# Sliding-window attention and token MLP in one program: all score masks on GpSimd, key and query buffers per head group, and small matmuls between the first transposes

## The chip, the core and the metric

The kernel runs on one core of one Trainium2 chip. The metric is device time in microseconds for one execution. Three runs of the kernel before took 444.39 (the median), 444.18 and 446.07 us.

## The reference

The input is x, one sequence of 2048 tokens of 512 features, in bf16. Two layers follow, with the same weights, and each has two parts:

```
x = x + A(layernorm(x), wqkv, wo)          # sliding-window attention
x = x + B(layernorm(x), w1, b1, w2, b2)    # MLP over the tokens
```

A has 32 heads of 16 features. Query i sees key j if 0 <= i - j < 256; scores are scaled by 1/4, masked, put through a softmax and multiplied with v, and the heads go through wo. B normalises x again and mixes over the tokens: `u = gelu(einsum("bsd,sf->bdf", h, w1) + b1)` with 1792 hidden units, `y = einsum("bdf,fs->bds", u, w2) + b2`, and y is transposed back and added to x.

## The kernel before

x stays in SBUF as 16 token tiles of 128 rows. Four such tiles make a block m of 512 tokens, and 64 tokens make a "64-block"; keys and queries are counted in 64-blocks.

**Recording and order.** The kernel is recorded as a graph of operations (`Graph.op`), each with an engine, a function, what it reads and writes, and in some cases other engines that could do it (`alts`). `ORDER` is a packed list, found ahead of time by a planner, that gives for every operation its place in the program's order and which of its engines does it. `replay` goes through the list and hands out buffers from pools; `emit` works out the semaphore waits. So each engine's queue holds its operations in the order of that list, and an engine that waits holds up all that stands behind on it.

**Attention.** `qkv(m, ...)` transposes the normalised tiles of a block (on TensorE with `ident` for the first blocks, line 570, copied out by ACT or DVE at 577/579; by DMA for the others), projects keys, queries and values (line 534, a helper of all large matmuls), and copies them out. Keys go into `kbd`, which has zeros wherever a row belongs to the other head of a pair (its slots 1 and 2 are zeroed by the two memsets of line 482, on GpSimd); for m > 0 this takes a copy to `stg` (614) and a multiplication by `par`, on GpSimd or DVE, or DMAs (629). The buffers `qT` (2 slots) and `kbd` with `vb` (3 slots) are held by block: one slot has all four head groups o.

`attention(qs, nq, ...)` handles a chunk of nq 64-blocks of queries, head group by head group (eight heads each). A chunk's scores are packed into score tiles after `attention_plan`. For each score tile TensorE writes four row-tiled sets of scores (710) into four PSUM banks, ACT makes two exponentials of 128x1024 from them into `pt` (736; seven `pt` buffers), and the product with v follows on TensorE (774). Its result is transposed on DVE (794), divided (798 and 800, the latter on GpSimd or DVE), transposed again (805), and goes through wo (534) into x (816). Layer 0 has the chunks (0,4), (4,4), (8,8), (16,8), (24,8), layer 1 the chunks (0,8), (8,8), (16,8), (24,8).

**Masks.** The edges of the window are masked in one of two ways:

- on GpSimd (757): after the exponential, `pt` is multiplied in place by `ldm`, an int32 matrix of zeros and ones;
- on TensorE (721), for the score tiles that `BIASED` names: a large negative number is added to the scores in PSUM by 8 or 16 more matmuls of `sel` and `bb`, ahead of the exponential. `sel` and `bb` are made at the start by one memset (457) and twelve short DVE instructions (465 and 472).

```
BIASED = [{1: (0, 1), 2: (2, 4), 3: (2, 4)}, {}]
```

That is: in layer 0, chunk 1 has tiles 0 and 1 of each head group biased, chunks 2 and 3 have tiles 2 and 4; in layer 1 no tile is.

**Around the attention.** Layer norms take their statistics on DVE (492, 494), the power -1/2 on GpSimd (505, `rstd`) and the scaling on DVE (512, `xh_sb`). While the attention of a chunk runs, TensorE also has the projections of later blocks, wo, and the first part of the token MLP, u = xh^T w1 (`u_part`, 534, with its evictions 880 to 884); in layer 1 also y = u^T w2 of layer 0 (`y_block`, 534 and 936). What is left of u is done after the last chunk (`u_last`, 895, 906 and 910), and layer 1 ends with its own y.

**Start.** `f_warm` issues 42 matmuls of 128x128 on ones while x is loaded (395). x tiles 0 and 1 are then normalised one at a time, transposed, and projected by halves of a block.

Of the kernel before, what the change touches and what calls it, by code (L numbers as in the profile page):

```python
# [11 lines left out]
P = 128  # L12
# [3 lines left out]
    'c-p;HKZx_l6(4zLzti5$7bY-;K9~!0puiNmpaTUI(18Lf6i^|84jgdd!Urx~xX^(L6)IG?Foy~k3aD_QfD02`nBc;N3kO`daIuApEnIA|#THv^v4x9_*WO+4'  # L16
    '?zeYelH;ELNSb*wn)iFZ_j?rAF$R-hFaQl1MD2Rqc6z-ObQ9Q0I+5N0tsfxQJZ;LS!FS>l^i3OrI;cSnFmiiGyf&@5jmh6O=dO2NTm8i)OK$V|W~Nxg7^#NJ'
    'jjxzWMnhGW85~ZB!%dnDi#TCwz^U3X`=CE6K9r;3hd+J&A?k2$x9mn-Z`d_2@O-X0ys9W)ZDu~_p3arkO4F#KBpQtoqCinF!l<RHmyDTgyH(T%p_c@!H#fEo'
    'NVc*z7gx)rZQEqE`f@g-o6U?;v>FcifYR~k?(U8nMQON*e0lM;b<<dPEWE%=X9dwLoN9=Vo17!WSnl--R;v{`8+g1d*>cJ3@O|9YvQTV@`f(kFjD=AUgsre$'
    'mjA9V@Th3F+et!`s7Pp0q!H~kBfshgxY=lUp55>Wvn;<FRI61LU0q#Y-QCqLYZ$k#WABm}OV6p{>GYd_jSO=bcu3bBr;09vC~|ja!lu#fqK=_h3gbLjuXRIT'  # L20
    'a!#pfo0flZVL8syS+3A~GSdksh!<QHCs)g&$TCEfZLfz>#~TpkdUG||B%9m2+h+6bE_+|=tk>7K7_G*e%|()&uk6*#j?BWIPUot6bv2)_*K2Q>=l1z>B&XKg'
    'DyRL~yx;HJqp?r^Zjx_F+3)wVtoP?$-ox0o`(-~>Rof^i<(RQv7KT|Cwma9?##N_f7`!dZ?W!Eqo6V-Gaxd@!cT|~DS=Togx=zl|?Un7?OUKb<O`D9@OKwg$'
    '?qil?Sx)`T_iKsZPm=VbJa==KQf6B`HlsMHitSt~JG!h9g`8o_rj#1mnrfOxu!7Gf>dus*pyxPd;&??bw|cg!&;-S?5ow{JzsFe9G4C}pzhS5}U?O*xYML_R'
    '8dE5vf`XLl(`koLQ*e|6?M|uHY8uyded}y3Sw7SC1u$>c*Yh==&mq(h!o$<S_U>*7Zjp>Jl7)3rC=5s-ALRKKH=ENe&+`%3&7?8_zQ3WWtI8m5M2;{Bk^ngl'
    'u$o#GL7@4_b2+yR1^@)8FvHAj119Rkvcv#&b;cFWn8J346i_Hu$1|92=?jbMq~kh{m{1W|VJu$GCON?XqtwsUIE&-Bu4z#fQ4JHMAm5K7U*KTbwp9fHdjbMV'
    'm&;26=ks%@Y4&(V`NSIIdn>*ITkt_fc^F1#XR_REbUFyir@DR`*6Xz(2&&)LzpmFcSckGqF?3zzpPtDO%!F+@EEl#lzj2)5(CO6DG_BRTjYit&h(c>Sx^8M7'
    'htT&_)3FTz08v#!bO0e&i6l#g$OIN%rb*E4?d>%}NM9@#=bMcHSJj7;;dwe9t0PSt2wV$I^RnFc7(36h)k-OUTmGZk{ZU~GpbE0JQ?=wWjO%rs>)%n4GNv*Y'
    'Lc6t+<;M3LzFfBX`U0>1fEJ6AfmuFSET@ZtF)%La7=UrJ2}bqls8$1kBfBekI9yD1IoC9)>}SFOj}XB)>-O&;>=#KQb)_uIFt)O!i_H<nol=i1p%7CTg;_Q0'
    'R<c$%%i19boodag1MYfGvs(2;O5JL;&W8hs*K0x|8jS5K%drEYKECS%lQ^cR_49K_t6C6ZHqrg*G`PGBdIcD(*Ur_|KQ->yg7K=U8pdW5U)WKkYjLcGmTQS3'
    'Y1ok+;?~ubt{M98&jG)^k^R43se(cm4O(9<mkUbgA|q{8`Jnu6P>x0;H*hDO=eW~yOrW#SEK!i<e7-39L=mLw!SPO_I-R2YvUibQ;=EVIdEmO^F&=l_K~|=e'  # L30
    'h6%<7fr!}k_%@Dx&#hkgLCaq{#72&72SH5;RW)l?P1p5=*t%{IP=D)r)Kgs7kY)Ws5RZrsQC(8gFm6Xw9y_)xi(Uu?J2g!)Wzb@A+<>9RDO6~k)l{|sz?*Kj'
    'TQr#f{n{ZIsVtYNyqGT~!Twn~o6g`VoQy@F(QpU`Vdy2jZjx2{{Z<jhu4Q$_TV$gnhwUKsyk@<oyKW^-JvWKH7)Hp}bwg+m)OEpco3_~*L`|+jRfdoPfe^%w'
    'wS{mxxfBm~7Tv5j&AhAteYMi<RVrGaZjHw0<Kb#)>3Ugy^G%)`gP~}g3P_5qAU}XMwBN^;l{gDG-^oeXj^fDr_FLcgEVOZb&oSjc8W2DNA)>SZLZ?PIK;j7l'
    'Qr1ghFHL|@tDV{aAbYckswh+eghG(brY&u}U5oM(!bJiy8YAH(8b#T!*TsLm=vxM8Hd{?SYBZV+N-zYnnYeM1c1$OAfnkV3HUiVqEV+PyF;T;YX%Wj7osI~x'
    'u||Zr!or0s8lTYN8=WwPh{O=l-U(4|ZZH=n<VSd8;UHvwm<T-yhf_9TO!Qbfh@uFtI-M}g$E;H(JPgyc*G(tA-e?rxcGEN|Hk(l1xe3_;j?;7+;sM$1&=!f1'
    '<)9SSGVF%vL%<G9A<eqsIEI0c2*I!o3ur3P02T3LfOata684$+Jlearyrld5>~D|m-*!K&d2&8nPL78p>Evlc@pSJXZ1;co?$^9N*ZmYcsZ`!oo{jH4Pag&='
    'A3tBE@;E8pdV0U)*)gAjl>{r{{(RyG@2?O@$A0jz&(Q{llZ(;Mjy+F~A$ljBoV*C?4JeOMl)xU=hZjl@FRq*(N4$%$a)|R)^al^=kfz72KAObm=Xgc|Ns>N+'
    'VL#(@Qh95pa#E>$5{IS7xSp6LNtMIRBO9e-8t;7`;@?9Gq{r~2iX<JURC=D@r<#yHHChS$s`i^tb9?`jvz2=q9jax|s7I*3c=C9>JS}@8bEo&PL-55Hp9Ao@'
    'bfD5bxCdgtqSS$<(lL^vBq4lMf)nuKcBdR?JN?*~)QMQU7n*xzd8uE*Pd))}7s|6Lsys)ca#U=)%kF!xr=L}h)>Xg(5a}&q+)q5kBos$H?67(Fv}!-Q`;*?i'
    '+YRmp#1DcOT67PCw8u#Vzencu<mBxV1g|EghtpR+0?6y9O64)ehj1$|rMB|AmmHKtdaH`0=jsOzJbAGkNXJ?wN&i#HNv}mvdXQO3l3o&VuO5;FB<WZM_JdD)'  # L40
    '@^Ie6*zxGW@v-~8Ao)*pub+?PztWmVG5>#5{FgB4r{5%j2gDxiS@nEeiho_z{SPfNNM8'
# [52 lines left out]
class Graph:  # L94
# [4 lines left out]
    def __init__(self, nc, es):  # L99
        self.nc = nc  # L100
        self.sem = {e: es.enter_context(nc.semaphore(f"s_{e}")) for e in self.ENGS}
        self.dsem = [es.enter_context(nc.semaphore(f"s_dma{i}")) for i in range(self.NDMA)]
        self.ops = []
        self.last_w = {}
        self.readers = {}

    def op(self, eng, fn, reads=(), writes=(), cost=200.0, prio=None, dma=False, after=(), holds=(), cfg=None, cls=None,
# [197 lines left out]
def bass_interleave_layers__sliding_block__mixer_token_mlp__prompt_kernel(  # L305
# [19 lines left out]
    MASKED = 4e9  # L325
# [5 lines left out]
    BIASED = [{1: (0, 1), 2: (2, 4), 3: (2, 4)}, {}]  # L331
# [4 lines left out]
    with es:  # L336
# [22 lines left out]
        sel = sb("sel", [P, 2, P])  # L359
        bb = sb("bb", [P, 2, 4, 64])  # L360
# [17 lines left out]
        p_xhT, p_qT, p_stg = Pool("xhT", 2), Pool("qT", 2), Pool("stg", 5)  # L378
        p_kv, p_pt, p_rl, p_oT = Pool("kv", 3), Pool("pt", NPT), Pool("rl", NRL, True), Pool("oT", 2)
# [76 lines left out]

        op("gpsimd:zero", lambda e: e.memset(sel[:].rearrange("p a b -> p (a b)").bitcast(dt.float32), 0.0), writes=["sel"], cost=200)
        BIAS_KEYS = []
        for r in range(4):
            g0, g1 = 32 * r, 32 * r + 32  # L460

            def f_sel(e, g0=g0, g1=g1):
                d, v = sel[g0:g1, 0, 0:32], ident[g0:g1, g0:g1]
                (p, c), (q, _) = [[list(a) for a in x.ap] for x in (d, v)]
                return e.tensor_copy(bass.AP(d.tensor, d.offset, [p, [160, 2], [64, 2], c]),
                                     bass.AP(v.tensor, v.offset, [q, [0, 2], [0, 2], c]))
            op("vector:sel", f_sel, reads=["ident", "sel"], writes=[("sel", r)], cost=150)
            for i, (add, mul) in enumerate(((-1.0, MASKED), (0.0, -MASKED))):
                def f_bb(e, g0=g0, g1=g1, i=i, add=add, mul=mul):
                    v = tri[g0:g1, g0:g0 + 64]  # L470
                    p, c = [list(a) for a in v.ap]
                    return e.tensor_scalar(bb[g0:g1, :, 2 * i:2 * i + 2, :], bass.AP(v.tensor, v.offset, [p, [32, 2], [0, 2], c]), add, mul,  # L472
                                           op0=ALU.add, op1=ALU.mult)
# [542 lines left out]
```

## Time and profile before

| | |
|---|---|
| median of three runs | 444.39 us |
| the profiled execution: own time, span | 445.56 us, 443.6 us |
| time outside the span | 1.96 us |
| TensorE / VectorE / ScalarE / GpSimd busy | 418.5 / 307.4 / 322.7 / 201.1 us |
| mean granted TensorE clock | 0.996 |
| exponentials (736) | 304, spaced 0.93 us where they run back to back |
| layer 0's exponentials | from 11.1 to 158.5 us |
| layer 1's exponentials | from 207.0 us on; the last masks begin at 361.9 us |
| masks on GpSimd (757) | 226 instructions, 149.9 us by the groups of their shapes |
| mask matmuls on TensorE (721) | 352, from 21.7 to 117 us |

PE is TensorE, PEld its weight loads, DVE VectorE, ACT ScalarE, POOL GpSimd, SP the queue that issues DMAs. L736 is line 736 of the kernel. Matmuls overlap and their ends are modelled, so PE's busy share says less than the moment at which the next instruction starts.

### The profile page before, as it was taken

To read this page: it belongs to the slowest core of one execution; us is meant where nothing else is said; L and a number is where in the kernel's file an instruction comes from. 1 tells how busy PE (TensorE), PEld (TensorE's weight loads), DVE (VectorE), ACT (ScalarE), POOL (GpSimd) and SP (SyncE) were. 2 spreads that over 40 slices of the span, in tenths; PEclk is the share of its full clock that TensorE was granted. 3 is DMA by queue.
4 is the path that set the end of the run, shared out by engine and by line. 5 is a ranking of instruction groups with operands and counts; after the bars stand their busy time and mean duration, and the time that the engine had idled before them with its cause. 6 is when DMAs were issued, how large, how long until landed. Compare 5 with 4: busy or idle time off the path is not lost.

```text
span 443.6 us, 14491 instructions
## 1 busy us (share of the span) xinstructions
PE 418.5 (94%) x6270; PEld 193.5 (44%) x6344; DVE 307.4 (69%) x582; ACT 322.7 (73%) x372; POOL 201.1 (45%) x305
## 2 busy tenths in 40 slices
PE   7888988998999999999999999999999999999997
PEld 5554443443443444444444444444334444444443
DVE  7988879777895678664468789898887457521223
ACT  3999999999999940708989999999999980430000
POOL 3567652464577641001456686677866551000000
PEclk8999999999999999999999999999999999999999
DMA  7575504410133538451434434031211347653533
GB/s 242 153 129 91 101 16 72 77 28 18 36 83 100 122 88 249 125 168 25 99 80 104 111 73 97 17 71 38 56 45 30 105 123 202 189 158 99 167 115 105
DMA packets 94127, 44.47 MB, mean 100 GB/s; under 512 B 24304, under 2 KB 94064, under 8 KB 94064
## 3 DMA queue, kind: packets, MB, share of 16 engines
q1 hardware_dynamic: 94064, 43.55, 39.1%
q8 instruction: 50, 0.82, 0.8%
q14 instruction: 13, 0.11, 0.1%
HBM read 33.56 MB, written 2.10 MB: 80 GB/s over the span
## 4 chain that ended last, share of the span: by engine, by line
PE 79%; ACT 13%; DVE 3%; issue 2%; DMA 1%; SPq 1%; POOL 1%; POOLq 0%
PE PS L534 53%; ACT pt L736 12%; PE PS L710 9%; PE PS L895 8%; PE PS L774 8%; DMA w1b<-in_B_w_dram 1%; DVE rl L794 1%; PE PS L721 1%; DVE stats L492 1%; SPq L830 1%; PE PS L570 0%; DVE vst L649 0%; DVE bb L472 0%; DVE x_sb L816 0%; POOL rstd L505 0%
## 5 line engine op out<-in xcount | busy, mean ns | idle before, releaser
L736 ACT ACTIVATE pt<-PS 128x1024 bf16<-128x1024 f32 (+1 forms) x304 | 281.9, 1034 | 12.0 <-PE PS L710 8.0
L757 POOL TENSOR_TENSOR pt<-pt,ldm 128x256 int32<-128x256 int32 (+2 forms) x226 | 146.9, 675 | 91.7 <-ACT pt L736 91.2
L534 PE MATMUL PS<-xhT,wqkv 128*128 128x512 bf16 (+1 forms) x267 | 65.3, 362 | 4.5 <-issue 1.4
L534 PE MATMUL PS<-xh_sb,w1b 128*128 128x512 bf16 x262 | 66.0, 380 | 2.9 <-issue 1.9
L534 PE MATMUL PS<-uT,w2b 128*128 128x512 bf16 (+1 forms) x285 | 66.7, 370 | 0.8 <-issue 0.5
L710 PE MATMUL PS<-qT,kbd 32*128 32x256 bf16 (+4 forms) x1488 | 60.4, 252 | 5.6 <-ACT pt L736 2.8
L936 DVE SCALAR_TENSOR_TENSOR x_sb<-PS,b2col,x_sb 128x512 bf16<-128x512 f32 x31 | 22.4, 745 | 48.4 <-PE PS L534 48.4
L505 POOL TENSOR_TENSOR rstd<-agg,mhalf 128x2 f32<-128x2 f32 (+1 forms) x33 | 23.5, 713 | 67.8 <-DVE agg L494 67.8
L794 DVE STREAM_TRANSPOSE rl<-PS 128x1024 f32<-128x1024 f32 x32 | 39.9, 1246 | 19.8 <-PE PS L774 19.3
L710 PEld LDWEIGHTS PS<-qT,kbd 32*128 32x128 bf16 x1488 | 22.0, 93 | 63.9 <-ACT pt L736 48.2
L774 PE MATMUL PS<-pt,vb 64*17 64x320 bf16 (+4 forms) x2976 | 43.6, 252 | 1.2 <-DVE vst L649 0.5
L910 ACT ACTIVATE uT<-rl,b1col 128x512 bf16<-128x512 f32 x28 | 18.5, 713 | 36.1 <-DVE rl L906 35.7
L492 DVE BATCH_NORM_STATS2 stats<-x_sb 128x6 f32<-128x512 bf16 x64 | 42.8, 678 | 0.4
L534 PEld LDWEIGHTS PS<-uT,w2b 128*128 128x128 bf16 x294 | 27.1, 98 | 30.9 <-issue 3.7
L534 PE MATMUL PS<-uT,pt 128*128 128x512 bf16 x163 | 39.5, 380 | 0.3
L774 PEld LDWEIGHTS PS<-pt,vb 64*17 64x17 bf16 x2976 | 31.0, 85 | 17.4 <-issue 7.3
L895 PE MATMUL PS<-xh_sb,w1b 128*128 128x512 bf16 x164 | 37.0, 379 | 0.7 <-DMA w1b<-in_B_w_dram 0.6
L534 PEld LDWEIGHTS PS<-xh_sb,w1b 128*128 128x128 bf16 x280 | 23.8, 98 | 31.6 <-issue 7.0
L534 PEld LDWEIGHTS PS<-xhT,wqkv 128*128 128x128 bf16 x288 | 24.5, 99 | 28.8 <-issue 5.6
L534 PE MATMUL PS<-wqkv,xhT 128*128 128x512 bf16 x115 | 32.3, 381 | 3.5 <-issue 1.3
L534 PE MATMUL PS<-wo_sb,oT 128*128 128x512 bf16 x124 | 32.6, 380 | 0.4 <-issue 0.3
L512 DVE TENSOR_SCALAR xh_sb<-x_sb,agg,rstd 128x512 bf16<-128x512 bf16 x64 | 27.2, 445 | 3.2 <-POOL rstd L505 3.1
(64 smaller groups left out, 337.0 us busy)
## 6 DMA issues: line engine op xcount, KB each, us to landing
w1b<-in_B_w_dram SPq DMA_DIRECT2D x112, 128.0 KB, 2.7
w2b<-in_B_w_dram SPq DMA_DIRECT2D x70, 128.0 KB, 2.6
pt<-in_B_w_dram SPq DMA_DIRECT2D x42, 128.0 KB, 3.2
vb<-vst SPq DMA_DIRECT2D x64, 68.0 KB, 2.1
out_dram<-x_sb SPq DMA_DIRECT2D x15, 128.0 KB, 1.8
x_sb<-in_A_x_dram SPq DMA_DIRECT2D x3, 512.0 KB, 7.3
wqkv<-in_A_wqkv_dram SPq DMA_DIRECT2D x4, 256.0 KB, 4.5
wqkv<-in_A_wqkv_dram SPq DMA_DIRECT2D x1, 512.0 KB, 6.6
```

Of the source, the lines that this page charges most:

```text
L492: op("vector:stat", lambda e: e.bn_stats(st[:, 0:6], x_sb[:, t, :]), reads=[f"x{t}"], writes=[("st", i)], cost=dve_cost(512))
L505: op("gpsimd:rstd", lambda e: e.tensor_tensor(rstd[:, t0:t1, 0], agg[:, t0:t1, 1], mhalf[:, 0:1].to_broadcast([P, t1 - t0]), op=ALU.pow), ...
L512: op("vector:xh", lambda e: e.tensor_scalar(xh_sb[:, t, :], x_sb[:, t, :], agg[:, t, 0:1], rstd[:, t, :], op0=ALU.subtract, op1=ALU.mult), ...
L534: return e.matmul(o, lhsT=w, rhs=x, start=start, stop=stop, skip_group_check=True)
L710: last = e.matmul(bank(tt[r // 2], r % 2)[:, base + c0 * 64:base + (c0 + n) * 64], lhsT=kbd[32 * r:32 * r + 32, tk.slot, o, jj].rearrange( ...
L736: op("scalar:exp", lambda e, ts=ts, tp=tp, i=i, cols=cols: e.activation(probs(tp)[:, i, 0:cols, :], pair(ts)[:, :, 0:cols].rearrange("p r ...
L757: return e.tensor_tensor(v, v, m, op=ALU.mult)
L774: last = e.matmul(bank(t, h)[32 * r:32 * r + 17, i + q0 * 64:i + (q0 + n) * 64], lhsT=vb[64 * h:64 * h + 64, tk.slot, jj, 4 * o + r, :], r ...
L794: op("vector:od", lambda e, t=tod, tr=tr: e.transpose(rl[:, tr.slot:tr.slot + 2].rearrange("p a b -> p (a b)"), pair(t)), reads=[(tod, i) ...
L895: last = e.matmul(bank(tu, tt), lhsT=v()[:, sc - b0, k0 + tt * P:k0 + (tt + 1) * P], rhs=xh_sb[:, sc, :], start=(sc == b0), stop=(sc == NT ...
L910: op("scalar:gelu", lambda e, ft=ft, tt=tt: e.activation(uT[:, ft, :], rl[:, tmps[tt].slot], ACTF.Gelu_apprx_tanh, bias=b1col[:, ft:ft + 1 ...
L936: op("vector:resy", lambda e: e.scalar_tensor_tensor(x_sb[:, t, :], bank(ft), b2col[:, t:t + 1], x_sb[:, t, :], op0=ALU.add, op1=ALU.add), ...
```

## The change

- **Masks.** `BIASED`, `sel`, `bb`, the biased matmuls, and the memset and twelve DVE instructions that make `sel` and `bb` are gone. All score tiles are masked on GpSimd.
- **Buffers.** `qT` becomes a pool of 8 slots of one head group each, `kbd` one of 12; `vb` keeps 3 slots by block in a pool of its own. The memory is the same; a slot is free again once its own head group has been used.
- **Warm-up.** `f_warm` issues 40 matmuls instead of 42. After the transposes of x tile 0 come 2 more matmuls of the same kind, after those of tile 1 come 8 (`keep_warm`); the TensorE operation that is recorded next has to follow them.
- **Zeroing.** The two memsets of `kbd` are recorded after the first layer norms and read `xh1`, so they can't run ahead of tile 1's scaling.
- **Order.** `ORDER` is another list, for the new graph.
- In `u_part` and `u_last` two expressions are written more generally; with the splits in use they give what they gave before.

```
...
-    'c-p;HKZx_l6(4zLzti5$7bY-;K9~!0puiNmpaTUI(18Lf6i^|84jgdd!Urx~xX^(L6)IG?Foy~k3aD_QfD02`nBc;N3kO`daIuApEnIA|#THv^v4x9_*WO+4'
+    'c-qBPKZxtd86Vl>yLp`6p@Vs#g9+$h4wNtfB`84w6$%VN50s$7g$`Ue;D8DhE?l@!zyTF598lrHg$oxhT&PgtfCw%&u*DWGT)1$+g^Mj5aIuApEw;$m>s@>I'
...
+        if eng == "tensor":
+            after, self.next_pe = list(after) + self.next_pe, []
         for a in after:
             deps[a.idx] = a
...
-    BIASED = [{1: (0, 1), 2: (2, 4), 3: (2, 4)}, {}]
...
-        qT = sb("qT", [P, 2, 4, 512])
+        qT = sb("qT", [P, 8, 512])
         stg = sb("stg", [P, 5, 512])
-        kbd = sb("kbd", [P, 3, 4, 8, 2, 64])
+        kbd = sb("kbd", [P, 12, 8, 2, 64])
...
-        p_xhT, p_qT, p_stg = Pool("xhT", 2), Pool("qT", 2), Pool("stg", 5)
-        p_kv, p_pt, p_rl, p_oT = Pool("kv", 3), Pool("pt", NPT), Pool("rl", NRL, True), Pool("oT", 2)
+        p_xhT, p_qT, p_stg = Pool("xhT", 2), Pool("qT", 8), Pool("stg", 5)
+        p_k, p_v, p_pt, p_rl, p_oT = Pool("k", 12), Pool("v", 3), Pool("pt", NPT), Pool("rl", NRL, True), Pool("oT", 2)
...
-            for _ in range(42):
+            for _ in range(40):
                 last = e.matmul(PS[:, warm.slot, 0:P], lhsT=uT[:, 0, 0:P], rhs=uT[:, 0, 0:P], start=True, stop=True)
             return last
+        def keep_warm(n, after):
+            spare = Tile(banks)
+
+            def f(e):
+                for _ in range(n):
+                    last = e.matmul(PS[:, spare.slot, 0:P], lhsT=uT[:, 0, 0:P], rhs=uT[:, 0, 0:P], start=True, stop=True)
+                return last
+            g.next_pe = [op("tensor:fw", f, reads=["uT0"], writes=[spare], cost=60 * n, cfg="f", cls="f", after=after)]
...
-        op("gpsimd:zero", lambda e: e.memset(sel[:].rearrange("p a b -> p (a b)").bitcast(dt.float32), 0.0), writes=["sel"], cost=200)
...
-            op("vector:sel", f_sel, reads=["ident", "sel"], writes=[("sel", r)], cost=150)
...
-                op("vector:sel", f_bb, reads=["tri"], writes=[("bb", r, i)], cost=150)
...
-        for k in (1, 2):
-            op("gpsimd:zero", lambda e, k=k: e.memset(kbd[:, k].rearrange("p a b c d -> p (a b c d)").bitcast(dt.float32), 0.0),
-               writes=["kz0"], cost=1900)
...
+        def zero_keys():
+            for k in (1, 2):
+                op("gpsimd:zero", lambda e, k=k: e.memset(kbd[:, 4 * k:4 * k + 4].rearrange("p a b c d -> p (a b c d)").bitcast(dt.float32), 0.0),
+                   reads=["xh1"], writes=["kz0"], cost=1900)
...
-            tx, tq, tk = Tile(p_xhT), Tile(p_qT), Tile(p_kv)
+            tx, tq, tk, tv = Tile(p_xhT), [Tile(p_qT) for _ in range(4)], [Tile(p_k) for _ in range(4)], Tile(p_v)
...
+                if wide and not layer and m == 0:
+                    keep_warm((2, 8)[i], [g.ops[-1]])
...
+                if first and not layer:
+                    zero_keys()
...
-                    on_pe = su[0][0] in biased and len(su) == 1
-
-                    def f_sc(e, su=su, tt=(tA, tB), on_pe=on_pe):
-                        last, fresh = None, True
+                    def f_sc(e, su=su, tt=(tA, tB)):
...
-                        for c0, nc_, w0 in plan[su[0][0]][1] if on_pe else ():
-                            for a in range(2):
-                                lo = 32 if w0 < 2 and a else 0
-                                hi = nc_ * 64 - (32 if w0 + nc_ > 2 and not a else 0)
-                                for r in range(4):
-                                    last = e.matmul(
-                                        bank(tt[r // 2], r % 2)[:, c0 * 64 + lo:c0 * 64 + hi],
-                                        lhsT=sel[32 * r:32 * r + 32, a, :],
-                                        rhs=bb[32 * r:32 * r + 32, 1 - a].rearrange("p i n -> p (i n)")[:, w0 * 64 + lo:w0 * 64 + hi],
-                                        start=False, stop=True, tile_position=(32 * r, 0), skip_group_check=True)
...
-                    masks, mk = [] if on_pe else list(plan[su[0][0]][1]), []
+                    masks, mk = list(plan[su[0][0]][1]), []
...
```

More of the change, by code (lines that the diff above doesn't have):

```diff
@@ L609, in proj @@
                     op(two[0][0] + ":evka", two[0][1], reads=[key] + [("par", h) for h in range(2)],
-                       writes=[(tk, "k", o, h, k) for h in range(2) for k in KEYS(a, b)], cost=two[0][2], prio=-3e5, alts=two[1:])
+                       writes=[(tk[o], h, k) for h in range(2) for k in KEYS(a, b)], cost=two[0][2], prio=-3e5, alts=two[1:])
                     if wide:
@@ L619, in f_kz @@
                     got = []
-                    assert layer or m > 2 or tk.slot
+                    assert layer or m > 2 or tk[o].slot > 3
                     for h in range(2):
@@ L955, in bass_interleave_layers__sliding_block__mixer_token_mlp__prompt_kernel @@
                 phase[0] = 8 * layer + c
-                tos[c] = attention(qs, nq, tqs, tks, BIASED[layer].get(c, ()))
+                tos[c] = attention(qs, nq, tqs, tks)
                 gate.append([prev_sc[0]])
```

115 lines of the change are left out of this document (48 added, 67 removed).

## The prediction

> **What bounds the kernel now.** I read the page first, then the busy time by stages, the groups of line 721 and 757, the list of waits, and the start in order of time.
>
> ```profile
> span 443.6 us, 14491 instructions
> PE 418.5 (94%) x6270; PEld 193.5 (44%) x6344; DVE 307.4 (69%) x582; ACT 322.7 (73%) x372; POOL 201.1 (45%) x305
> ...
> ACT  3999999999999940708989999999999980430000
> POOL 3567652464577641001456686677866551000000
> ```
>
> ACT is at 9 through both attention stages and nearly empty elsewhere; POOL's 45% is an average over stages of 70% and stages of nothing. So the stages are read apart (columns: window, its length, then busy us of each engine):
>
> ```profile
> 16.00:66.00 50.00, 43.67 (x1147) 23.32 (x1157) 42.49 (x88) 47.77 (x55) 34.68 (x47) 1.00 0.46 81
> 66.00:133.00 67.00, 62.40 (x1338) 27.82 (x1350) 56.31 (x106) 65.48 (x71) 33.17 (x51) 1.00 0.25 52
> 260.00:310.00 50.00, 48.73 (x859) 21.00 (x868) 44.38 (x81) 47.26 (x52) 36.83 (x56) 1.00 0.25 53
> 286.00:297.00 11.00, 10.63 (x195) 4.74 (x190) 10.53 (x19) 9.83 (x11) 10.01 (x14) 1.00 0.36 78
> ```
>
> Layer 0's attention (16 to 133) is set by ACT: 96 to 98% busy, PE 87 to 93%. In layer 1 (260 to 310) PE is at 97% and ACT at 95%. The last row is a stretch of layer 1 in which four engines all run at 89 to 97%.
>
> ```profile
> L757 POOL TENSOR_TENSOR pt<-pt,ldm 128x256 int32<-128x256 int32 x162 | 117.8, 743 | 57.4 <-ACT pt L736 56.8
> L757 POOL TENSOR_TENSOR pt<-pt,ldm 128x128 int32<-128x128 int32 x60 | 28.2, 472 | 30.7 <-ACT pt L736 30.7
> L721 PE MATMUL PS<-bb,sel 32*128 32x96 bf16 x256 | 7.8, 201 | 0.0
> ```
>
> These groups give the prices of masks (mean ns after the comma). Of the waits, the first line is from 11 to 160 us, the second from 310 to 365, where every mask is on POOL:
>
> ```profile
> ACT pt L736 <- PE PS L721: 2.7, 9, 0.6
> ...
> PEld PS L774 <- POOL pt L757: 2.0, 5, 0.5
> ```
>
> The start: projections at 7.60 and, for comparison, twelve equal ones at 18.85; and the clock by half microseconds (PE busy, then PEclk).
>
> ```profile
> 7.60 2.74 PE L534 MATMUL PS<-xhT,wqkv 128*128 128x256 bf16 x12 [0.68 <-ACT xhT L579]
> ...
> 18.85 1.49 PE L534 MATMUL PS<-xhT,wqkv 128*128 128x256 bf16 x12
> ...
> 7.00:7.50 0.50, 0.00 (x0) 1.00 1.05 313
> 7.50:8.00 0.50, 0.40 (x3) 0.59 1.05 301
> ...
> 10.50:11.00 0.50, 0.50 (x13) 0.50 1.16 352
> 11.00:11.50 0.50, 0.50 (x6) 1.00 1.01 356
> ```
>
> The granted clock is halved from 7.59 to 11.0 us, and the first projections take 2.74 us instead of 1.49. In the chain that ended last, they stand between the copy of the transposes and ACT's first keys and exponentials, after which ACT hardly stops: its delay at the start goes to the end of layer 0's attention.
>
> **The change part by part**, against the profiled execution (span 443.6, own time 445.56, so 1.96 outside; 1.17 above the median of 444.39).
>
> (a) Small matmuls. If the clock holds, 2.74 - 1.49 = 1.25 us leave the chain. In the 3.41 us before the drop (4.18 to 7.59) PE was busy for 1.68, with no gap over 0.68. The windows row 56.2 to 59.6, 2.19 busy of 3.40, kept the full clock. The last of the 42 matmuls ran 10 in half a microsecond, so ten more make some 0.5 and two fewer in front take 0.1: about 2.1 busy, close to the row that held. Against: eight at 0.05 to 0.1 us need 0.4 to 0.8 in a gap of 0.67, so up to 0.2 late. From -1.25 to +0.2; I take -0.8. The Trainium skill, "TensorE: Matmul & The Clock Gate", Part 1, says that the clock falls after an idle window of about 3.4 us; read literally, nothing fell here for idleness and the ten matmuls are worth nothing (the sum would be 0.8 higher). The row speaks against that reading: it halved at half-busy.
>
> (b) Mask matmuls gone. 352 of them, 8 or 16 behind the scores of 24 tiles: chunk 1 has 4 x 8 + 4 x 16, chunks 2 and 3 have 8 x 16 each. From the first of 16 to the next instruction is 0.29 us (69.00 to 69.29), of 8 it is 0.19 (27.97 to 28.16): 20 x 0.29 + 4 x 0.19 = 6.6 us of PE. ACT waited 2.7 us for them in nine places; some of these waits go over to the scores themselves (line 710), so ACT gets 2.0 (from 0 to 2.7), and layer 0's attention ends that much earlier.
>
> (c) The other 4.6 of the 6.6 us count only where TensorE's later work (u, projections) is pulled into the gaps, shortening the PE-bound stretch after ACT's last exponential. PE already has 6.3 + 4.6 us of gaps from 16 to 133 that the present order leaves open. Between 0 and -4.6; half, -2.3.
>
> (d) Masks added to POOL. Chunk 1, for each of four head groups: two of 256 columns and one of 128, so 4 x (2 x 0.743 + 0.472) = 7.8 us; chunks 2 and 3: 8 tiles each with two of 256, 2 x 8 x 1.486 = 23.8. Together 44 instructions and 31.6 us. They hide beside ACT, but POOL is a strict queue: behind each mask stand `rstd`, the products (800), the key copies (629), and for them DVE's scaling and the next block's projections; PE's products with v wait for the mask itself. Price from below: in layer 1, 138 masks from 209 to 362 us cost PE's weight loads 2.4 us (the 2.0 shown, and 0.4 from 260 to 310), so 44 cost 0.8; below zero is excluded, since a mask can't come before its exponential. From above: from 16 to 66 us POOL has 34.7, and gets chunk 1's 7.8 and five tiles of chunk 2, 7.4: 49.9 of 50. It has to give its eight key copies and four products to DVE, which is at 42.5. The two together: 92.4 of 100. Layer 1 held 20.5 of 22 (93%) for 11 us, but 81.2 of 100 over 260 to 310. At the latter rate, 92.4 take 56.9 us instead of 50: +6.9. I take +1.2, near the low end, for work there isn't tied to that stretch: from 66 to 133 POOL would have 33.2 + 16.3 of 67, and key copies and statistics of blocks 2 and 3 can go there.
>
> (e) The twelve DVE instructions for `sel` and `bb` take 2.7 us, most beside the loading of x; four lie in the crowded stretch from 9.9 to 15.3. From -0.8 to 0; I take -0.3. Without that cover nothing is lost.
>
> (f) Buffers by head group, and the two memsets (1.80 us each): in the list of waits nobody waits for a slot of `qT` or `kbd`, and the memsets already start at 16.72 and 29.73, long after tile 1's scaling (6.06). Zero; if a memset is put ahead of an `rstd` or a mask, 1.8 is late once.
>
> (g) The new order reaches everywhere. In layer 1, 209 to 362, PE is idle 4.7 of 153 us: gaining more isn't in the rows, losing as much is easy. 0, with 4.7 to both sides.
>
> Sum: -0.8 - 2.0 - 2.3 + 1.2 - 0.3 = -4.2. Span 439.4, own time 441.4, median 440.2.
>
> **The rivals.**
>
> *POOL and DVE full from 16 to 66 us (slower).* Then (d) costs 6.9; of (b) and (c) only what lies outside that stretch stays, about 1.3; the start keeps 0.8. 444.4 + 6.9 - 2.1 = 449.2. It decides as soon as the two engines together can't hold 93% for 50 us. For it: DVE's own instructions get longer beside masks: `xh_sb` took 384 ns from 66 to 133 us and 509 from 260 to 310, the DVE key copy 345 and 531. The Trainium skill, "SBUF — State Buffer", "Who interferes with whom", gives such a lock between the two engines; it speaks against this change, and the rows agree. Against: the 11 us row, with PE at 97% beside it.
>
> *ACT alone sets the end (no change).* ACT's 2.7 us of waits turn into others, PE's freed time stays idle: 444.4 - 0.8 - 0.3 + 0.8 = 444.1. For it: the gaps that PE has today in a stage where ACT is at 96%. Against: the 9.6 us of u that is still done after 156 us (44 matmuls at 0.22), and could move up.
>
> *All of it is used (faster still).* -1.25 - 2.7 - 4.6 + 0.8 - 0.3 = -8.05: 436.3. It needs a filler for every gap.
>
> If the change doesn't do what it says, it is in (a): the clock falls all the same, and the forecast ends at 441.0.
>
> **How the numbers follow.** Forecast 0.49 (its own range 437.5 to 442.1), all of it used 0.13, no change 0.14, POOL and DVE full 0.24. A measurement of this kernel tells about 0.5% (2.2 us). Faster 0.62, same 0.14, slower 0.24. The range goes from 435, below the best case by a little of (g), to 449.5, just over the slow one; some 0.06 lies below and 0.12 above.
>
> **What would show it.** Right: clock 1.00 from 7.5 to 11 us, ACT's first exponential before 10.3; no L721; 270 masks and some 233 us on POOL; products and key copies of 16 to 66 us mostly on DVE; ACT's last exponential of layer 0 near 155 us; PEld waiting under 5 us for masks. Wrong: PEld or ACT waiting for masks or `rstd` by more than that before 133 us, layer 0's attention as long as before (147.4 us), or a longer layer 1, where nothing was changed but the order.

## The result, and the profile after

The changed kernel takes 445.71 us (median of 20 executions; 444.43 to 448.72), the kernel before 444.33 (443.78 to 446.07). The ratio is 1.0034, with a 95% interval from 1.0019 to 1.0048: slower by about a third of a per cent. The forecast was 440.2. The profiled execution after has an own time of 445.6 and a span of 443.8.

The page of the changed kernel, with ACT and POOL in forty slices:

```profile
span 443.8 us, 13856 instructions
PE 415.2 (94%) x5930; PEld 188.7 (43%) x6000; DVE 301.8 (68%) x557; ACT 323.3 (73%) x374; POOL 234.7 (53%) x351
...
ACT  3888999999999931637999999999999970530000
POOL 5577887677996731010665758976896651000000
```

POOL has its 33.6 us more (the forecast said 31.6), PE lost 3.3 busy us. By stages, in the windows of before (length, then busy us of PE, PEld, DVE, ACT, POOL, then the granted clock, the DMA share and GB/s):

```profile
16.00:66.00 50.00, 41.89 (x927) 19.68 (x936) 43.64 (x92) 45.73 (x54) 38.42 (x57) 1.00 0.44 94
66.00:133.00 67.00, 59.56 (x1209) 25.14 (x1211) 57.27 (x101) 66.42 (x73) 53.63 (x79) 1.00 0.33 70
260.00:310.00 50.00, 48.42 (x857) 20.68 (x865) 39.71 (x73) 48.12 (x54) 40.00 (x61) 1.00 0.23 51
286.00:297.00 11.00, 10.47 (x177) 4.43 (x176) 10.45 (x18) 10.00 (x12) 9.18 (x14) 1.00 0.40 88
```

The new order put 26 of the 44 added masks between 66 and 133 us (POOL 53.63, before 33.17) and 17 between 16 and 66. From 66 to 133 ACT is busier than before, 66.42 against 65.48. From 16 to 66 it is less busy, 45.73 against 47.77: there lies what layer 0 loses. The masks' groups, and the waits from 11 to 160 us for a mask and of ACT:

```profile
L733 POOL TENSOR_TENSOR pt<-pt,ldm 128x256 int32<-128x256 int32 x202 | 146.5, 745 | 38.9 <-ACT pt L712 38.6
...
L733 POOL TENSOR_TENSOR pt<-pt,ldm 128x128 int32<-128x128 int32 x64 | 30.1, 472 | 15.7 <-ACT pt L712 13.0 <-DVE ldm L459 2.6
```

```profile
PEld PS L750 <- POOL pt L733: 3.3, 8, 0.5
...
ACT pt L712 <- PE PS L697: 4.0, 7, 1.3
ACT qT L582 <- PE PS L520: 1.4, 1, 1.4
```

A mask costs what it did (745 and 472 ns), and TensorE waits for masks for only 3.3 us. But ACT waits 5.4 us where it waited 4.4: the 2.7 us for line 721 are gone, and waits for scores (L697) and projections (L520) of up to 1.4 us have come. At the start the clock holds:

```profile
7.06 0.60 PE L520 MATMUL PS<-xhT,wqkv 128*128 128x256 bf16 x4
8.14 1.05 PE L520 MATMUL PS<-xhT,wqkv 128*128 128x256 bf16 x8 [0.49 <-DMA wqkv<-in_A_wqkv_dram]
```

```profile
7.50:8.00 0.50, 0.15 (x2) 0.00 (x0) 0.41 (x3) 0.31 (x1) 0.24 (x1) 1.00 0.95 298
10.50:11.00 0.50, 0.50 (x6) 0.29 (x3) 0.49 (x2) 0.50 (x2) 0.19 (x1) 1.00 1.27 207
```

Twelve projections take 0.60 and 1.05 us, and the first exponential starts at 9.73 instead of 11.11. So 1.38 us are won at the start and lost again by 20 us. All engines in order of time (start, duration), shortly after:

```profile
13.54 2.12 DVE L493 TENSOR_SCALAR xh_sb<-x_sb,agg,rstd 128x512 bf16<-128x512 bf16 x1
13.70 1.80 POOL L499 MEMSET kbd<- 128x2048 f32 x1
...
15.71 0.40 PE L556 MATMUL PS<-ident,xh_sb 128*128 128x128 bf16 x4 [0.16 <-DVE xh_sb L493]
...
17.36 0.73 DVE L565 COPY xhT<-PS 128x512 bf16<-128x512 bf16 x2
...
18.15 1.05 PE L520 MATMUL PS<-xhT,wqkv 128*128 128x256 bf16 x8 [1.46 <-DVE xhT L565]
18.80 0.37 ACT L582 CAST qT<-PS 128x256 bf16<-128x256 f32 x1 [1.38 <-PE PS L520]
```

The scaling of x tile 3 takes 2.12 us; the same instruction takes 0.40 for the tile before it. It ends 0.16 us after the memset of `kbd` that started beside it. The view of busy time counts these 1.7 us as DVE's work, so no wait of DVE shows them. Transposes, their copies, the projections and ACT (idle 1.38) follow late. Later ACT waits another 1.34 us, at 32.80, for scores that stand on TensorE behind projections of block 1, whose transposes come by DMA.

The spans of the profiled executions, cut at the exponentials, put the rest in place (us, differences of rows of the timelines; "to layer 1" runs from layer 0's last exponential to layer 1's first):

| kernel | first exp. | layer 0 exp. | to layer 1 | layer 1 exp. | to the end | span |
|---|---|---|---|---|---|---|
| before | 11.11 | 147.39 | 48.54 | 154.11 | 82.45 | 443.6 |
| old order, small matmuls | 9.87 | 147.35 | 48.05 | 154.06 | 82.47 | 441.8 |
| old order, 24 tiles unmasked | 9.61 | 144.94 | 48.38 | 154.25 | 82.52 | 439.7 |
| old order, masks on POOL | 9.78 | 155.90 | 48.51 | 154.09 | 82.42 | 450.7 |
| after | 9.73 | 148.26 | 47.86 | 154.37 | 83.58 | 443.8 |
| after, memset moved | 8.97 | 146.30 | 47.86 | 154.36 | 84.11 | 441.6 |
| after, three moves (below) | 9.06 | 146.00 | 47.86 | 154.43 | 83.35 | 440.7 |

### The profile page after: what moved, and what is told of

Same layout as the page of the kernel before. It is cut to its first block, busy times and chain, and to the rows that moved or that the text cites. A ratio compares the mean times of both kernels' runs of the same rounds, so it can differ in the third digit from the quotient of the medians.

```text
span 443.8 us, 13856 instructions
## 1 busy us (share of the span) xinstructions
PE 415.2 (94%) x5930; PEld 188.7 (43%) x6000; DVE 301.8 (68%) x557; ACT 323.3 (73%) x374; POOL 234.7 (53%) x351
## 4 chain that ended last, share of the span: by engine, by line
PE 65%; ACT 21%; DVE 5%; DMA 2%; issue 2%; SPq 2%; POOL 1%; DVEq 0%
PE PS L520 46%; ACT pt L712 21%; PE PS L697 7%; PE PS L871 6%; PE PS L750 6%; DMA wqkv<-in_A_wqkv_dram 1%; POOL pt L733 1%; DVE rl L770 1%; DVE xh_sb L493 1%; SPq L818 1%; DMA w1b<-in_B_w_dram 1%; SPq L806 1%; DMA pt<-in_B_w_dram 1%; DVE rl L882 0%; DVE qT L580 0%
## 5 line engine op out<-in xcount | busy, mean ns | idle before, releaser
L733 POOL TENSOR_TENSOR pt<-pt,ldm 128x256 int32<-128x256 int32 (+2 forms) x270 | 177.2, 684 | 57.6 <-ACT pt L712 54.6
L520 PE MATMUL PS<-xhT,wqkv 128*128 128x512 bf16 (+1 forms) x273 | 64.4, 355 | 8.0 <-ACT pt L712 4.1
L520 PE MATMUL PS<-uT,w2b 128*128 128x512 bf16 (+1 forms) x285 | 69.3, 369 | 1.1 <-issue 0.5
L520 PE MATMUL PS<-xh_sb,w1b 128*128 128x512 bf16 x262 | 65.8, 380 | 3.3 <-issue 1.7
L697 PE MATMUL PS<-qT,kbd 32*128 32x256 bf16 (+4 forms) x1488 | 60.3, 251 | 5.9 <-ACT pt L712 3.0
L697 PEld LDWEIGHTS PS<-qT,kbd 32*128 32x128 bf16 x1488 | 22.0, 92 | 64.1 <-ACT pt L712 48.4
L520 PE MATMUL PS<-uT,pt 128*128 128x512 bf16 x162 | 41.4, 379 | 0.6 <-DMA pt<-in_B_w_dram 0.3
L520 PEld LDWEIGHTS PS<-uT,w2b 128*128 128x128 bf16 x294 | 26.9, 98 | 31.7 <-issue 4.0
L520 PEld LDWEIGHTS PS<-xhT,wqkv 128*128 128x128 bf16 x288 | 24.2, 97 | 34.3 <-ACT pt L712 5.7
L520 PEld LDWEIGHTS PS<-xh_sb,w1b 128*128 128x128 bf16 x280 | 23.6, 97 | 32.6 <-issue 6.4
L493 DVE TENSOR_SCALAR xh_sb<-x_sb,agg,rstd 128x512 bf16<-128x512 bf16 x64 | 32.0, 519 | 4.4 <-POOL rstd L486 4.3
L520 PE MATMUL PS<-wqkv,xhT 128*128 128x512 bf16 x117 | 31.8, 380 | 2.3 <-ACT pt L712 1.1
L520 PE MATMUL PS<-wo_sb,oT 128*128 128x512 bf16 x120 | 30.9, 380 | 1.6 <-issue 1.0
```

The lines of the kernel that those rows point to most:

```text
L493: op("vector:xh", lambda e: e.tensor_scalar(xh_sb[:, t, :], x_sb[:, t, :], agg[:, t, 0:1], rstd[:, t, :], op0=ALU.subtract, op1=ALU.mult), ...
L520: return e.matmul(o, lhsT=w, rhs=x, start=start, stop=stop, skip_group_check=True)
L697: last = e.matmul(bank(tt[r // 2], r % 2)[:, base + c0 * 64:base + (c0 + n) * 64], lhsT=kbd[32 * r:32 * r + 32, tk[0][o].slot, jj].rearran ...
L733: return e.tensor_tensor(v, v, m, op=ALU.mult)
```

## The experiments

My theory: most of the loss is the memset beside the scaling, with what follows from it. The rivals: the masks on POOL after all, and the new order in itself. In the runs on the old order, its list is kept and only what a part adds or drops is changed in it. The buffers by head group have no run of their own; they are in the run with every part. Medians are set against the kernel before on the same chip ("+" is slower).

**The parts by themselves, in the old order.** Small matmuls alone (40 in front, then 2 and 8):

```
-            for _ in range(42):
+            for _ in range(40):
+                if wide and not layer and m == 0:
+                    keep_warm((8, 2)[i], [g.ops[-1]])     # tile 1 is transposed first here
```

> The kernel before with its own order, plus the small matmuls: 40 instead of 42 at the start, 2 after the transposes that run first, 8 after those that run second. Theory A (the start is worth its time, and the new order loses it again further on): the clock stays at 1.00 from 7.5 to 11 us, the first exponential comes 1.0 to 1.4 us earlier than 11.1, and 0.8 to 1.4 us of that reach the end: 443.0 to 443.6 against 444.3. Theory B (a later start of nothing else: the gain at the start is taken up by the next wait, the weights' DMA or DVE): first exponential earlier, end within 0.4 us of before.

Measured: 444.23, -0.4 us, ratio 0.9988 (0.9978 to 0.9999). The first exponential starts at 9.87, but two kernels without small matmuls, next, start theirs at 9.61 and 9.78: the halved clock of before's profile is not in every execution. Of 99 executions of before beside these runs, 23 had a mean granted clock of 0.996 and a median time of 445.35, the other 76 had 0.999 or 1.0 and a median of 444.20.

No masks for the 24 tiles, so that the 352 mask matmuls leave and nothing comes in their place (these scores stay unmasked):

```
-                    masks, mk = [] if on_pe else list(plan[su[0][0]][1]), []
+                    masks, mk = [] if bare else list(plan[su[0][0]][1]), []   # bare: the 24 tiles; sel, bb and on_pe are gone
```

> The kernel before with its own order, with the masks of the 24 biased tiles left out altogether: no mask matmuls, no GpSimd masks for them. This is what the freed PE time is worth without any price on GpSimd. The prediction's steps (b) and (c) together were 4.3 us (0 to 7.3). If ACT alone sets the end of layer 0's attention: 0 to 2.7 us faster (ACT's waits for line 721), the rest of the 6.6 us turning into PE idle time. If PE's time counts: 4 us or more faster.

Measured: 441.71, -2.9, ratio 0.9929 (0.9914 to 0.9944). Layer 0's exponentials take 144.94 us, 2.4 less. The next stretch is no shorter (48.38).

The 24 tiles masked on POOL, each mask in the list behind the second ACT instruction after its exponentials:

```
-                    masks, mk = [] if on_pe else list(plan[su[0][0]][1]), []
+                    masks, mk = list(plan[su[0][0]][1]), []
```

> The kernel before with its own order, but the 24 tiles' masks on GpSimd: 44 mask instructions put in behind the next tile's exponentials, 352 matmuls and the 13 instructions for sel and bb left out. Theory A (masks on GpSimd are about free, the loss of the changed kernel is in its order): 443.3 to 444.8. Rival 1 (POOL and DVE full from 16 to 66 us): slower by 3 to 7 us, with waits of PE for masks and rstd there. Rival 2 (ACT alone sets the end of layer 0): within 0.7 us of before, last exponential of layer 0 still at 158 to 159.

Measured: 451.97, +7.4, ratio 1.016 (1.014 to 1.018). All engines in order of time at one of the places:

```profile
112.50 1.37 POOL L604 TENSOR_SCALAR kbd<-stg,par 128x512 bf16<-128x512 bf16 x2
...
113.83 2.79 POOL L718 TENSOR_TENSOR pt<-pt,ldm 128x256 int32<-128x256 int32 x4
...
115.39 0.93 PE L735 MATMUL PS<-pt,vb 64*17 64x64 bf16 x56 [2.07 <-POOL pt L718]
...
118.32 1.94 ACT L697 ACTIVATE pt<-PS 128x1024 bf16<-128x1024 f32 x2 [3.30 <-PE PS L682]
```

A key copy stands ahead of four masks, the product with v waits 2.07 us for one of them, the next scores stand behind that product on TensorE, and ACT is idle for 3.30. It is a burst: from 112.50 to 116.62 POOL is full, and over the whole stage it is not (45.35 us busy from 66 to 133). Behind it the granted clock is halved from about 116 to 119.4 us, so the 3.30 hold some of that as well. Of the 12.2 us that ACT waits for scores up to 168 us, 8.4 lie between 66 and 133, not from 16 to 66 where the rival had put them.

The same with the 44 masks cut to 8 of their columns (the rest of these scores stays unmasked), and, at full width, with each mask directly behind its exponential in the list:

```
-                        def f_mask(e, tp=tp, w=nc_ * 64,
+                        def f_mask(e, tp=tp, w=8 if short else nc_ * 64,
```

> b_pool with the 44 added masks cut to 8 columns each (the rest of those tiles' masks is left out): the same instructions at the same places in GpSimd's queue and the same waits, but little GpSimd time. If b_pool's 7.4 us are GpSimd's time: most of it goes, 441.7 to 443.5. If they are the extra step between exponential and product, however short: 447 or more.

> b_pool with the 44 added masks put into GpSimd's queue directly behind their own tile's exponentials, ahead of key copies and products that stood in front of them. If b_pool's loss is the place of the masks in GpSimd's queue: at least 3 us faster than b_pool's 452.0. If GpSimd has too little time in layer 0 whatever the place: within 1.5 us of b_pool, with other work late instead.

Measured: 443.07 (-1.4; 0.9962, 0.9948 to 0.9976) and 471.55 (+27.0; 1.0602, 1.0584 to 1.062). Against the kernel without these masks, 44 nearly empty instructions cost 1.5 us, their full width 8.8 more, and an earlier place in POOL's queue another 20. There, each mask holds up whatever POOL could have done while its exponential was still running: POOL waits 49.6 us for exponentials up to 175 us, against 28.0 up to 168 with the later place. Neither expectation had that. How much of the 20 is the queue and how much the clock stays open: the clock is also halved for 27 us in all, and its mean is 0.971 to 0.974 in all four executions (0.996 to 0.999 with the later place).

Every part together (masks on POOL, buffers by head group, small matmuls) in the old order:

> Every part of the change, but in the order of before: masks on GpSimd put in as in b_pool, small matmuls as in b_warm, buffers by head group. Theory A (the new order is what loses): 442.3 to 443.8, the sum of b_warm and b_pool, so 2 to 3 us less than the changed kernel's 445.7. Rival (the parts lose in any order): 445 or more.

Measured: 452.4, +7.8, ratio 1.0174 (1.0154 to 1.0193), like the masks alone. So the new order, at +1.4, has won back 6.4 of 7.8 us; as a whole it is not what loses, and the second rival is left with single places in it.

**In the new order.** The changed kernel with `masks = []` for the 24 tiles, so without its 44 added masks:

> The changed kernel with its own order, with the 44 added masks left out of GpSimd's queue (those tiles go unmasked). If the masks still cost time in the order that was found for them: 1.5 us or more faster than the changed kernel's 445.7, down to b_nomask's 441.7. If the new order hides them and loses elsewhere: 445 to 445.7.

Measured: 446.47, +2.0, ratio 1.0031 (1.0012 to 1.0051), the same as the changed kernel's 1.0034 (and above what was expected either way). In the new order the masks cost nothing that can be measured: the first rival falls for this order. The long scaling, 2.12 us beside the memset, is in this kernel too.

The second memset placed behind the next three masks, nothing else, in two runs:

```
 [rstd 2] ... [mask 0]
-[memset kbd 2]
 [mask] [mask] [mask]
+[memset kbd 2]
 [rstd 4]
```

> The changed kernel with one instruction moved: the second memset of kbd, which starts at 13.70 us while the scaling of x tile 3 on DVE (13.54) takes 2.12 us instead of 0.4, goes behind the next three masks on GpSimd (about 17.3 us). If DVE was held by the memset and that stall is on the path: the scaling is back at 0.4 us, ACT's idle time of 1.38 at 18.80 goes, and 0.8 to 1.4 us reach the end (444.3 to 444.9). If it isn't on the path: the scaling is short, the end unchanged within 0.4.

> The changed kernel with the second memset behind the next three masks, run a second time with the other three on one chip. The memset theory: again some 2 us below the changed kernel, 443.0 to 444.2. The rival, that its first runs were lucky in the clock: 445 to 446.

Measured: 443.66 (-0.85; 0.9991, 0.9964 to 1.0017) and 444.42 (+0.35; 1.0002, 0.9981 to 1.0022); in the profiled execution of the first:

```profile
12.78 0.40 DVE L493 TENSOR_SCALAR xh_sb<-x_sb,agg,rstd 128x512 bf16<-128x512 bf16 x1
...
15.69 1.81 POOL L499 MEMSET kbd<- 128x2048 f32 x1
...
15.89 1.05 PE L520 MATMUL PS<-xhT,wqkv 128*128 128x256 bf16 x8 [0.30 <-DVE xhT L565]
```

The scaling is back at 0.40, and TensorE's wait of 1.46 is 0.30. Against the changed kernel's +1.38 the move is worth 2.2 us by the medians in the first run and 1.0 in the second, whose 444.42 lies between what was expected of the theory and of the rival, and whose interval overlaps the changed kernel's. The two differ because each median falls between two groups: in both runs six of twelve executions have a lowered clock, with medians of 445.98 and 445.77, and six have 0.999 or 1.0, with 442.13 and 442.84 (the changed kernel's four of that kind: 445.43). So at full clock the move is worth more than the medians say. In the profiled pair 0.76 of the 2.2 us of span come before the moved instruction (first exponential at 8.97 instead of 9.73, without the wait for wqkv); 1.96 come off layer 0's exponentials, and 0.5 are lost at the end.

The other way round: the old order with small matmuls, and the memset placed beside a scaling:

```
-               writes=["kz0"], cost=1900)
+               reads=[("bb", 1, 0)] if k == 1 else [], writes=["kz0"], cost=1900)
```

> The kernel before with its old order and the small matmuls, and one memset of kbd moved so that it begins together with the scaling of x tile 2 (it now reads the bb entry that DVE makes just ahead of that scaling). If a memset of 1.80 us holds DVE's scaling for its whole length, as the changed kernel's record suggests, the scaling takes 1.8 to 2.1 us instead of 0.41, that tile's transposes and ACT come 1.4 to 1.7 us later, and the time is 0.8 to 1.7 us above the kernel with the small matmuls alone (444.23): 445.0 to 445.9. Rival: the 2.12 us in the changed kernel came from something else (the exponentials' reads, the DMAs); then the scaling stays near 0.41 and the time is 444.0 to 444.6.

Measured: 445.78, +1.7, ratio 1.0039 (1.0025 to 1.0053), that is 2.1 us worse than the small matmuls alone (-0.4). First this kernel, then that one:

```profile
13.49 1.98 DVE L518 TENSOR_SCALAR xh_sb<-x_sb,agg,rstd 128x512 bf16<-128x512 bf16 x1
...
13.52 1.80 POOL L488 MEMSET kbd<- 128x2048 f32 x1 [2.77 <-DVE bb L478]
...
15.39 0.70 DVE L471 COPY sel<-ident 32x128 bf16<-32x128 bf16 x1
...
18.73 0.60 ACT L744 ACTIVATE pt<-PS 128x512 bf16<-128x512 f32 x1 [1.67 <-PE PS L718]
```

```profile
13.50 0.41 DVE L518 TENSOR_SCALAR xh_sb<-x_sb,agg,rstd 128x512 bf16<-128x512 bf16 x1
...
13.82 0.18 DVE L471 COPY sel<-ident 32x128 bf16<-32x128 bf16 x1
```

One memset of 1.80 us makes this one instruction 1.57 us longer. The next on DVE, a small copy, now falls beside a mask of 0.76 us and takes 0.52 longer. Together that is 2.1 us, and so is the difference of the medians (the profiled spans differ by 1.6). The time lies where the memset theory put it, and that settles the cause of this loss: it comes about in the old order too, with the small matmuls as the only other part of the change.

**The small matmuls, and TensorE's second wait.** The changed kernel without the ten small matmuls:

```
-            for _ in range(40):
+            for _ in range(42):
-                    keep_warm((2, 8)[i], [g.ops[-1]])
```

> The changed kernel without its ten small matmuls (42 in front again, the banks handed out as in the changed kernel). If they are worth in this order what they were in the old one, the median rises by 0.4 us, to about 446.1, and the profiled record shows either a halved clock before 11 us or none. Rival from the recorded forecast: they are worth 0.8 to 1.25 in every execution, 446.5 to 447.0. Third: in the new order they are worth nothing or cost their 0.2 us, 445.5 to 445.8.

Measured: 444.86, +0.8, ratio 1.0014 (1.0 to 1.0029). All three expectations put it above 445; in this order the ten matmuls bring nothing that can be measured.

Memset moved, and the scores of the twelfth score tile moved ahead of the two key projections that wait for block 1's transposes:

```
+[scores 11]
 [key projection, halves 1 and 2]
 ...
-[scores 11]
```

> The changed kernel with the second memset behind the next three masks, and with the scores of the twelfth score tile moved ahead of the two key projections that wait for block 1's transposes by DMA. In the kernel with the memset moved alone these projections start 1.68 us late, at 28.8 us, the scores behind them start at 29.56 and ACT stands idle for 0.81. If ACT's start carries to the end of layer 0, the idle time goes and the time is 0.5 to 0.8 us below that kernel: 442.8 to 443.2. Rival: ACT loses the time at its next wait, for the projections are late all the same, and the time stays at 443.5 to 443.8.

Measured: 442.95, -1.1, ratio 0.9977 (0.9958 to 0.9996). Ten of twelve executions lie between 441.61 and 443.9, two at 445.79 and 445.94. The profile caught one of these two; TensorE and ACT, then the granted clock (second number from the end but one):

```profile
27.96 0.40 PE L697 MATMUL PS<-qT,kbd 32*128 32x256 bf16 x8 [0.92 <-DVE rl L770]
29.92 4.43 PE L520 MATMUL PS<-xhT,wqkv 128*128 128x512 bf16 x10 [1.56 <-ACT pt L712]
...
34.94 1.94 ACT L712 ACTIVATE pt<-PS 128x1024 bf16<-128x1024 f32 x2 [3.99 <-PE PS L697]
```

```profile
28.00:28.50 0.50, 0.36 (x8) 0.08 (x8) 0.14 (x1) 0.50 (x2) 0.50 (x1) 1.00 0.60 138
28.50:29.00 0.50, 0.00 (x0) 0.00 (x0) 0.00 (x0) 0.50 (x2) 0.50 (x2) 0.68 0.18 35
29.00:29.50 0.50, 0.00 (x0) 0.00 (x0) 0.00 (x0) 0.50 (x2) 0.50 (x2) 0.50 0.07 10
```

In TensorE's wait the clock is halved, and ten projections take 4.43 us. The lowered clock is in two of twelve executions here, in 12 of 24 with the memset moved alone. To tell the clock from the wait, three more: 16 small matmuls ahead of those projections; wo's DMA issued behind block 1's four transposes instead of between them; and, in the changed kernel with nothing moved, 16 small matmuls in each of its two waits.

```
+                if again:                              # {(1, 1, 1, 0): 16}; the last one also {(0, 0, 2, 256): 16}
+                    op("tensor:fw", f_hot, reads=["uT0"], writes=[key], cost=60 * again, cfg="f", cls="f")
                 mm_group("fk" if which else "fq", key, 4, ...
```

> The kernel with the memset and the twelfth tile's scores moved, and 16 small matmuls ahead of the key projections that wait for block 1's transposes. In that kernel's record the clock is halved from 28.7 to 35.5 us behind this wait, the first eight projections take 3.57 us and ACT stands idle for 3.5; its executions are 441.6 to 443.9 with two at 445.8 and 445.9. If the halved clock makes those two and the matmuls hold it, all lie between 441.5 and 444 with a median of 442.3 to 442.8. Rival: they come from a transfer that lands late; then about one in six stays above 445, and the median is again 443.0.

> The kernel with the memset and the twelfth tile's scores moved, and the DMA of wo_sb, which SyncE issues between the first and the second of block 1's transposes (0.59 us of its queue), issued behind the fourth. If the queue of SyncE sets when the transposes land, the projections start up to 0.6 earlier, fewer executions lose the clock, and the median is 442.3 to 442.8. Rival: the transposes wait for the scaling of their x tiles on DVE, or for the transfers themselves, and the time is again 442.7 to 443.2.

> The changed kernel, its order and banks untouched, with 16 more small matmuls in each of TensorE's two long waits at the start: ahead of the projections that wait for x tile 3's transposes (about 17 us) and ahead of those that wait for block 1's transposes by DMA (about 29.5 us). Theory: besides the memset, the changed kernel loses in some of its executions because TensorE idles long enough there for the clock to be halved. Then the executions above 446.5 (4 of 20) go, the spread shrinks from 4.3 us to under 2, and the median is 445.0 to 445.5: the two waits themselves stay. Rival: the spread comes from the waits, that is from when the transfers land, and the matmuls change nothing: median 445.5 to 446, some executions above 447.

Measured: 443.01 (-1.45; ratio 0.9966, 0.9955 to 0.9976), all from 442.25 to 443.93; 443.02 (-1.44; 0.997, 0.9958 to 0.9983), one of twelve above 444; and 445.47 (+1.0; 1.0022, 1.0007 to 1.0038). In the first:

```profile
28.52 1.07 PE L579 MATMUL PS<-uT 128*128 128x128 bf16 x16
29.43 2.42 PE L520 MATMUL PS<-xhT,wqkv 128*128 128x512 bf16 x10
...
32.23 1.94 ACT L719 ACTIVATE pt<-PS 128x1024 bf16<-128x1024 f32 x2 [1.01 <-PE PS L704]
```

Ten projections take 2.42 instead of 4.43 us, ACT waits 1.01 instead of 3.99, and no execution is near 446 any more, with the median where it was: the halved clock made the tail of this kernel, not its median. None of 11 executions has a lowered clock with the matmuls, one of twelve (444.82) with wo's DMA moved. Against two of twelve that is too few to say what either edit does by itself; against 12 of 24, the three kernels with the scores moved (3 of 35) keep the clock more often, and all three beat both the kernel before and the changed one. The third run decides less than it was meant to. Its first 16 matmuls had to wait for the bank of the transposes, started at 16.99 instead of about 15.8, and in the profiled execution the clock was halved at 17.9 all the same; 4 of its 12 executions have a lowered clock, against 16 of 20 of the changed kernel. Its median is only 0.4 us better, by the runs of before beside each, and the changed kernel's four executions at full clock (445.25 to 445.6) lie about its median too: there the waits themselves make the loss. The clock isn't all of the spread either: three of the twelve still lie above 446.5, one of them (446.87) at full clock, and five of the changed kernel's executions with a lowered clock (444.43 to 445.01) are below all four at full clock. What else makes the spread was not traced.

## Why the prediction was wrong, point by point

The forecast was 4.2 us faster; measured is 1.4 slower. Three steps failed: (f), put at 0, made the kernel slower; (c), put at -2.3, brought nothing; and the 0.8 of (a) was not there to be won at the median.

**(a), and the step to the median: the start was counted twice.** I took 0.8 us off for the small matmuls and another 1.17 for the distance between the profiled execution and the median. But the two are largely the same thing: before's profiled execution, with a clock of 0.996, was one with the halved clock, of which the median execution has little or nothing (445.35 against 444.20 above). Step (a) had the mechanism right for that execution (-1.38 there), and the size wrong at the median: 0.4 in the old order, nothing measurable in the new.

**(b)** -2.0 was near: 2.4 us of layer 0's exponentials in the kernel without these masks, in the old order.

**(c)** -2.3 was wrong. Nothing was pulled forward. The large matmuls of line 534 (520 after) that start in each stage are the same (window, length, busy us and count of PE, then PEld; after comes first):

```profile
0.00:157.99 157.99, 88.39 (x379) 32.99 (x407) 1.00 0.42 96
157.99:205.85 47.86, 33.79 (x151) 14.68 (x153) 1.00 0.47 136
```

```profile
0.00:158.50 158.50, 89.61 (x374) 33.74 (x406) 0.99 0.40 89
158.50:207.04 48.54, 33.95 (x151) 14.66 (x153) 1.00 0.52 147
```

151 in the stretch before layer 1 in both (374 and 379 ahead of it are within what a trace may miss). The stretch is 47.86 us, against 48.05 in the old order with small matmuls. TensorE's freed time stayed idle, which is what the "no change" rival said of it. I had argued from gaps that existed, not from a filler that could be placed in them.

**(d)** +1.2 was near: nothing measurable in the new order. But the same 44 masks cost 10.3 us in the old one (+7.4 against -2.9), more than the 6.9 at my upper end, and for the most part not by the mechanism of the rival with POOL and DVE full: most of ACT's waits lie between 66 and 133 us, where the two hold 97 of 134. That rival's 92.4 us of 100 never came up: from 16 to 66 us the two have 82.1 after (43.64 and 38.42), since 26 of the masks went behind 66, and both memsets (3.6 us) and half of the key copies (2.9) left the stretch. Nor did key copies and products go to DVE, as I had written they would: over the whole run POOL kept 9 key copies of 24 and took 17 of 32 products (before 9 and 14), DVE went from 13 key copies to 9, and SyncE's DMAs from 2 to 6. What costs in the old order is the place in a strict queue, at bursts that an average over 50 us does not show. (The price from below was read from 138 masks; the trace has 136 from 209 to 362 us, which changes nothing.)

**(e)** was not measured by itself; it is in the -2.9 of the kernel without these masks, together with (b). From 9.9 to 15.3 us the record has five of the twelve instructions, not four.

**(f)** costed at 0, is the step that made the kernel slower: 1.0 to 2.2 us by the medians for one memset, which started at 13.70 where I had read 16.72 and 29.73 from the old order. I looked at who waits for the memset and when it starts at the earliest, and named only an `rstd` or a mask that could stand behind it in POOL's queue. The damage was to an instruction of another engine that waits for nothing. I had the mechanism in hand: the rival's evidence was that DVE's scaling gets longer beside masks (509 ns against 384). These are means: the medians are 406 and 404, and the longest are 810 and 412, so single instructions were held. The Trainium skill, "SBUF — State Buffer", "Who interferes with whom", says that `tensor_scalar` in a two-port mode and GpSimd exclude each other for a whole instruction; the 2.12 and 1.98 us beside 1.80 us of memset agree with that, and I had weighed it for masks only.

**(g)** 0, with 4.7 to both sides, held in size, and cost 1.4: layer 1's exponentials take 0.3 us longer than with the small matmuls in the old order, and from the last exponential to the end 1.1 longer (83.58 against 82.47). Waits for DMAs of w1 and w2 make 0.5 of that in the changed kernel (0.23 at 370.79 and 0.27 at 393.25); the rest was not traced further.

By the spans the account is this. Against the old order with small matmuls, both at a clock of 0.999 or 1.0, the changed kernel is 2.0 us longer: 0.9 in layer 0's exponentials, from which (b) should have taken 2.0, and the 1.4 of (g), less 0.3 in the other two stretches. Against the kernel without these masks, layer 0's exponentials take 3.3 us longer (148.26, 144.94). The memset makes 2.0 of them (146.30 once it is moved), the other two moves 0.3 (146.00); the last 1.1 stay open, and so does most of the 1.4.

With all three moves the kernel spans 440.7, the old order with small matmuls 441.8. Layer 0 ends 2.2 us earlier (155.06 against 157.22), 0.8 of it from an earlier first exponential, the stretch behind it is 0.2 shorter, layer 1 and the end are 0.4 and 0.9 longer. By medians this kernel, which is not the one of the forecast, is 1.44 us faster than before.

Of the signs I gave, right were the clock from 7.5 to 11, the first exponential (9.73), 270 masks, POOL's 234.7 us, and PEld's waits (3.3); but the first exponential comes as early without the small matmuls where the clock holds (9.61, 9.78), so this sign proved little. Wrong were the products and key copies, which did not go to DVE, and layer 0's attention, at 148.26 us as long as before; it was the sign I had named for a failure, though without the waits for masks that I had put beside it.

## What to carry to other kernels

When an instruction is moved on GpSimd, look not only at its own queue but at what DVE does beside it: a memset can stretch a short scaling to its own length, and the record shows that as busy time, so compare durations of the same instruction, not waits. When the profiled execution stands above the median, find out what it has that the median lacks before taking off both that and a gain at the same place. Where the executions of a kernel fall into two groups, compare group with group, since a median between them moves with their shares. Freed time of an engine is a gain only where a named instruction can move into it.

## What the runs showed of the hardware

- A memset of 1.80 us on GpSimd made a DVE scaling of 128x512 bf16 take 2.12 and 1.98 us instead of 0.40 and 0.41, although by the record it started 0.16 and 0.03 us ahead of the memset. A DVE copy of 32x128 bf16 took 0.70 us instead of 0.18 beside a mask of 0.76. DVE instructions that read PSUM took their usual time beside a memset: in before, at 16.72, copies of 0.69 and 0.41 us. So did two statistics, which read SBUF: 1.28 us at 15.75 with the memset moved.
- The clock is lowered in some executions and not in others of the same program: a mean of 0.996 in 23 of 99 of before. In the profiled executions it fell at 28.7 us after 3.4 us with some 2.05 us of TensorE work, and at 17.9 us nearly a microsecond after work had resumed, for 3.3 us or more each time; in before it fell after 1.68 us of work in 3.41, and held after 2.19 in 3.40.
